# Residual add: from an accumulating transfer back to VectorE, with the first unit's PSUM copies moved from ScalarE to VectorE

## The chip, the cores and the metric

The kernel runs on one core of one Trainium2 chip. The metric is the device time of one execution in microseconds, as the median of repeated runs. Before the change it is 324.42 us (three runs, 323.83 to 324.49). The profile below is of one such execution with a span of 322.4 us.

The engines have short names in the profile: PE is TensorE (matmul), PEld its weight loads, DVE is VectorE, ACT is ScalarE, POOL is GpSimd, SP is SyncE. [...]

## What is computed

A gated linear attention over four batches of 768 tokens, eight heads of 48 channels, and behind it a gated feed-forward layer with a residual:

```
for t in range(S):                         # state S is complex, a is the complex decay
    S_re, S_im = a[t] * S + k[t] v[t]^T    # the outer product is real
    y[t] = q[t] . S_re
x   = y as (3072 tokens, 384)
out = x + sigmoid(x @ w_res) * ((gelu(x @ w_gate) * (x @ w_val)) @ w_out)
```

The kernel replaces the recurrence by chunks. The decay is brought to logarithm and angle, both are summed over time with triangular matmuls, and q and k are scaled by exp(+sum), exp(-sum), and by cosine and sine of the angle sum. Each chunk of 128 tokens is then ordinary masked attention plus a carried state.

## The kernel before

A group `g` is 256 tokens (two chunks, C = 2). A unit is one or two groups: unit 0 is group 0, unit 1 is groups 1 and 2, and so on to unit 6, which is group 11. The program alternates two phases. Phase x(u) makes the exponentials, angles and sines of unit u+1, the logarithm steps of unit u+2, the second half of the attention of unit u and the output products of unit u-1. Phase y(u) makes the gate and value products of unit u with gelu, and begins the attention of unit u+1.

`weave` sorts the steps of several lists by a fraction of the phase, so a pair such as `(0.75, 0.8, ...)` says where in the phase a list of steps lies. Every activation and every table load goes through `act` or `table`, which chain them in the order of the text:

```
def tab(ins):
    if "tab" in T:
        tc.add_manual_dep(ins.ins, T["tab"].ins.name, order, reason="table order")
    T["tab"] = ins
```

The angle sum is reduced to turns, and VectorE takes its absolute value for the cosine by clearing the sign bit:

```
# cs_t(g, c): cs holds the angle sum in PSUM, fg[..., 1, :] the fraction, fg[..., 0, :] its magnitude
nc.vector.tensor_scalar(out=r, in0=cs3, scalar1=MAGIC, scalar2=MAGIC, op0=OP.add, op1=OP.subtract)
nc.vector.tensor_tensor(out=fg[:, hs, 1, :], in0=cs3, in1=r, op=OP.subtract)
if c == C - 1:
    nc.vector.tensor_scalar(out=fg[:, :, 0, :].bitcast(int32), in0=fg[:, :, 1, :].bitcast(int32),
                            scalar1=0x7FFFFFFF, scalar2=None, op0=OP.bitwise_and)
# p2_sin(g): two ACT Sin passes over fg give CS; products(g): DVE makes Q and K from CS
```

Attention copies the transposed q and k out of PSUM, one half on each engine, and casts the result; `xt_step` copies its transpose (cuts marked):

```
nc.scalar.copy(out=qk[0:DD, 0:512], in_=tp[0:DD, 0:512])
nc.vector.tensor_copy(out=qk[0:DD, 512:1024], in_=tp[0:DD, 512:1024])
...
x = xp.tile([128, DM], BF, tag="x", name="x")
nc.scalar.copy(out=x, in_=y)
...
if jj % 2 == 0:
    nc.scalar.copy(out=dst, in_=src)          # xt_step
else:
    nc.vector.tensor_copy(out=dst, in_=src)
```

The output step, once for each chunk of 128 tokens:

```
def op_step(u, jj):
    ...                                       # 12 matmuls into ps
    nc.vector.scalar_tensor_tensor(out=ot, in0=T["sg", u][:, jj], scalar=1.0, in1=ps, op0=OP.add, op1=OP.mult)
    t0 = token(u, jj) * 128
    if u == NU - 1:
        nc.vector.tensor_tensor(out=ot, in0=ot, in1=T["x", token(u, jj)], op=OP.add)
    nc.sync.dma_start(out=out[t0:t0 + 128, :], in_=ot)
    if u < NU - 1:
        nc.gpsimd.dma_start(out=out[t0:t0 + 128, :], in_=T["x", token(u, jj)], accum_op=OP.add)
```

GpSimd's queue also carries the loads of v and of the weights, and a small round trip through DRAM that turns one row of decays into a column. `decay0` and `decay2` write a row (`dm<-ar`, `dm<-E`, `dm<-Ei`) and read it back as `m`; `decay3` then makes M from it on VectorE. Groups 5, 7, 8, 10 and 11 use it; groups 1, 2 and 4 use a matmul instead.

The order of steps in the first phase x, which the change touches:

```
if u == 0:
    weave((0.0, 0.25, p1 of g1), (0.26, 0.3, csls), (0.31, 0.32, sm[0]), (0.35, 0.45, exs),
          (0.4, 0.64, p1 of g2), (0.641, 0.642, dec3), (0.645, 0.65, atn[:1]),      # atn[0] loads the table
          (0.65, 0.66, arctan of g1), (0.67, 0.85, cst), (0.75, 0.8, atn[1:]),      # atn[1:] is arctan of g2
          (0.9, 0.95, sin of g1), (0.96, 0.97, sm[1]), (0.0, 0.5, att))
```

Here g1 is the second unit (groups 1 and 2) and g2 the third (groups 3 and 4).

Of the kernel before, what the change touches and what calls it, by code (L numbers as in the profile page):

```python
# [12 lines left out]
OP = mybir.AluOpType  # L13
# [15 lines left out]
def kernel(  # L29
# [13 lines left out]
    nc = tc.nc  # L43
# [70 lines left out]
    T = {}  # L114
# [114 lines left out]
    def cs_t(g, c):  # L229
        s = g % NS  # L230
        th = T["th", g]
        if c == 0:
            T["fg", g] = pE.tile([128, C * H, 2, D], FP, tag="fg", name="fg")
        sl = slice(c * DM, (c + 1) * DM)
        cs = psM.tile([128, DM], FP, tag="mm", padded_shape=[128, 512], name="cst")
        nc.tensor.matmul(out=cs, lhsT=tmat[c], rhs=th[:, sl], start=True, stop=(s == 0))  # L236
        if s > 0:
            nc.tensor.matmul(out=cs, lhsT=ones2pi, rhs=T["P", g], start=False, stop=True)
        cs3 = cs.rearrange("p (h d) -> p h d", h=H)
        fg = T["fg", g]  # L240
        hs = slice(c * H, (c + 1) * H)
        r = pS.tile([128, H, D], FP, tag="r", name="r")
        nc.vector.tensor_scalar(out=r, in0=cs3, scalar1=MAGIC, scalar2=MAGIC, op0=OP.add, op1=OP.subtract)
        nc.vector.tensor_tensor(out=fg[:, hs, 1, :], in0=cs3, in1=r, op=OP.subtract)
        if c == C - 1:
            nc.vector.tensor_scalar(out=fg[:, :, 0, :].bitcast(mybir.dt.int32), in0=fg[:, :, 1, :].bitcast(mybir.dt.int32),  # L246
                                    scalar1=0x7FFFFFFF, scalar2=None, op0=OP.bitwise_and)

    def p2_sin(g):
        T["CS", g] = pQ.tile([128, C * H, 2, D], BF, tag="CS", name="CS")  # L250
# [76 lines left out]
    def attention(g, c):  # L327
        s = g % NS
        first = s == 0 and c == 0
        st = {}  # L330

        def Q(x):
            return T["Q", g][:, x].rearrange("p u d -> p (u d)")

        def K(x):
            return T["K", g][:, x].rearrange("p u d -> p (u d)")

        def V(h):
            return T["v", g][:, c, h]

        def grp(hg):
            def a():
                tp = psT.tile([128, 1024], BF, tag="tp", name="tp")
                for j in range(4):
                    x = c * H + hg * 4 + j
                    nc.tensor.transpose(out=tp[0:DD, j * 128:j * 128 + 128], in_=Q(x), identity=ident)  # L346
                for j in range(4):
                    x = c * H + hg * 4 + j
                    nc.tensor.transpose(out=tp[0:DD, 512 + j * 128:640 + j * 128], in_=K(x), identity=ident)  # L349
                qk = sqp.tile([128, 1024], BF, tag="qk", name="qk")  # L350
                nc.scalar.copy(out=qk[0:DD, 0:512], in_=tp[0:DD, 0:512])  # L351
                nc.vector.tensor_copy(out=qk[0:DD, 512:1024], in_=tp[0:DD, 512:1024])  # L352
                st["qk", hg] = qk
                at = psA.tile([128, 4, 128], FP, tag="at", name="at")
                for j in range(4):
                    nc.tensor.matmul(out=at[:, j], lhsT=qk[0:DD, 512 + j * 128:640 + j * 128],  # L356
                                     rhs=qk[0:DD, j * 128:j * 128 + 128], start=True, stop=True)
                atm = sqp.tile([128, 4, 128], BF, tag="atm", name="atm")
                nc.vector.tensor_tensor(out=atm, in0=at, in1=mask4, op=OP.mult)  # L359
                st["atm", hg] = atm  # L360
            return a

        def enter():
            if s == 0 or c > 0:
                return
            d = T["dk", g - 1][0:DD].rearrange("p (h d) -> p h d", h=H)
            Mb = T["M", g][0:DD].rearrange("p (h u) -> p h u", u=1).to_broadcast([DD, H, D])
            G = stt.tile([128, H, D], FP, tag="G", name="G")
            if s == 1:
                nc.vector.tensor_tensor(out=G[0:DD], in0=d, in1=Mb, op=OP.mult)  # L370
            else:
                nc.vector.tensor_tensor(out=G[0:DD], in0=d, in1=T["G"][0:DD], op=OP.add)
                nc.vector.tensor_tensor(out=G[0:DD], in0=G[0:DD], in1=Mb, op=OP.mult)
            Gb = stt.tile([128, H, D], BF, tag="Gb", name="Gb")
            nc.vector.tensor_copy(out=Gb[0:DD], in_=G[0:DD])
            T["G"] = G
            T["Gbf"] = Gb

        def dk():
            if s == NS - 1 and c == C - 1:  # L380
                return
            if c == 0:
                T["dk", g] = psD.tile([128, DM], FP, tag="dk", padded_shape=[128, 512], name="dk")
            d = T["dk", g]
            for h in range(H):
                nc.tensor.matmul(out=d[0:DD, h * D:(h + 1) * D], lhsT=K(c * H + h), rhs=V(h),
                                 start=(c == 0 and h == 0), stop=(h == H - 1), skip_group_check=True)

        def yy():
            y = psY.tile([128, DM], FP, tag="y", padded_shape=[128, 512], name="y")  # L390
            for h in range(H):
                ys = y[:, h * D:(h + 1) * D]
                hg, j = divmod(h, 4)
                nc.tensor.matmul(out=ys, lhsT=st["atm", hg][:, j], rhs=V(h), start=True, stop=first)  # L394
                if not first:
                    nc.tensor.matmul(out=ys, lhsT=st["qk", hg][0:DD, j * 128:j * 128 + 128],
                                     rhs=T["Gbf"][0:DD, h], start=False, stop=True)
            x = xp.tile([128, DM], BF, tag="x", name="x")
            nc.scalar.copy(out=x, in_=y)
            T["x", g * C + c] = x  # L400
            if c == 0:
                d = T["dk", g][0:DD].rearrange("p (h d) -> p h d", h=H)
                Gb = stt.tile([128, H, D], BF, tag="Gb", name="Gb")
                if s == 0:
                    nc.vector.tensor_copy(out=Gb[0:DD], in_=d)
                else:
                    nc.vector.tensor_tensor(out=Gb[0:DD], in0=d, in1=T["G"][0:DD], op=OP.add)
                T["Gbf"] = Gb

        def hi(f):  # L410
            def w():
                with tc.high_priority():
                    f()
            return w
        return [hi(f) for f in (enter, grp(0), dk, grp(1), yy)]


    def xt_step(u, jj):
        if jj == 0:
            T["xT", u] = xtp.tile([128, KD, 512], BF, tag="xT", name="xT")[:, :, 0:width(u)]  # L420
        tpx = psM.tile([128, DM], BF, tag="mm", padded_shape=[128, 1024], name="tpx")
        x = T["x", token(u, jj)]
        for f in range(KD):
            nc.tensor.transpose(out=tpx[:, f * 128:(f + 1) * 128], in_=x[:, f * 128:(f + 1) * 128], identity=ident)
        dst = T["xT", u][:, :, jj * 128:(jj + 1) * 128]
        src = tpx.rearrange("p (f t) -> p f t", f=KD)
        if jj % 2 == 0:
            nc.scalar.copy(out=dst, in_=src)
        else:
            nc.vector.tensor_copy(out=dst, in_=src)  # L430
# [28 lines left out]
    def op_step(u, jj):  # L459
        h2 = T["h2", u]  # L460
        ps = psM.tile([128, DM], FP, tag="mm", padded_shape=[128, 512], name="op")
        for ffi in range(KF):
            nc.tensor.matmul(out=ps, lhsT=h2[:, ffi, jj * 128:(jj + 1) * 128], rhs=wo[:, ffi, :],  # L463
                             start=(ffi == 0), stop=(ffi == KF - 1))
        ot = ob.tile([128, DM], FP, tag="ot", name="ot")
        nc.vector.scalar_tensor_tensor(out=ot, in0=T["sg", u][:, jj], scalar=1.0, in1=ps, op0=OP.add, op1=OP.mult)  # L466
        t0 = token(u, jj) * 128
        if u == NU - 1:
            nc.vector.tensor_tensor(out=ot, in0=ot, in1=T["x", token(u, jj)], op=OP.add)
        nc.sync.dma_start(out=out[t0:t0 + 128, :], in_=ot)  # L470
        if u < NU - 1:
            nc.gpsimd.dma_start(out=out[t0:t0 + 128, :], in_=T["x", token(u, jj)], accum_op=OP.add)  # L472


    def table(nm):
# [7 lines left out]
    def token(u, jj):  # L483
        return UNITS[u][0] * C + jj
# [23 lines left out]
    def phase_x(u):  # L508
# [34 lines left out]
        if u == 0:  # L543
            sm = [[call(sums, g) for g in gg if g % NS > 0] for gg in (g1, g2)]
            weave((0.0, 0.25, zip_steps([p1(g) for g in g1])), (0.26, 0.3, csls), (0.31, 0.32, sm[0]), (0.35, 0.45, exs),
                  (0.4, 0.64, zip_steps([p1(g) for g in g2])), (0.641, 0.642, dec3), (0.645, 0.65, atn[:1]),
                  (0.65, 0.66, [call(p1_arctan, g) for g in g1]), (0.67, 0.85, cst), (0.75, 0.8, atn[1:]),
                  (0.9, 0.95, sin), (0.96, 0.97, sm[1]), (0.0, 0.5, att))
            return
        if u == 1:  # L550
# [80 lines left out]
```

## Time and profile before

| what | value |
|---|---|
| time, median of 3 | 324.42 us |
| span of the profiled execution | 322.4 us |
| mean granted TensorE clock | 0.949 |
| DMA traffic | 34.55 MB, mean 107 GB/s |
| HBM read, written | 31.31 MB, 9.07 MB |
| accumulating transfers `out_dram<-x` | 22, 192 KB each, 3.7 us from issue to landing |
| stores `out_dram<-ot` | 24, 192 KB each, 2.5 us from issue to landing |

Busy time says how long an engine worked in a stretch, not whether the end waited for it. A stage's limit is read from what its engines waited for last. In a group's row the last column is the idle time of that engine just before those instructions, with the event that ended it. In the chain of waits each row is a start, a length and what the end of the program hung on at that moment. A timeline row gives start, duration, engine, line, operation, output and inputs, and in brackets the idle time before it. Instructions on one engine overlap a little in their records, so the distance from start to start, and not the duration, is what one more instruction takes from a busy engine.

### The profile page before, as it was taken

What the parts mean: (1) busy time and instruction counts of PE and PEld (TensorE: products, weight loads), DVE (VectorE), ACT (ScalarE), POOL (GpSimd) and SP (SyncE); (2) the same over time, 40 slices, a digit from 0 to 9 for tenths busy, and PEclk for the clock granted to TensorE, in tenths of its full rate; (3) what the DMA queues carried; (4) which work ended last, traced back from release to release, by engine and by line L of the source; (5) the groups of instructions that cost most, each with busy time, mean ns of one, the idle gap of its engine ahead of it and who ended that gap; (6) DMA issues with size and microseconds to landing.
All of it is one profiled execution on the core that took longest, in us unless ns stands there. A gap on an engine that the chain in (4) does not pass through costs nothing.

```text
span 322.4 us, 5853 instructions
## 1 busy us (share of the span) xinstructions
PE 272.1 (84%) x2200; PEld 170.5 (53%) x2200; DVE 234.8 (73%) x431; ACT 209.8 (65%) x353; POOL 80.5 (25%) x115
## 2 busy tenths in 40 slices
PE   0337927789887999789997999998999999899994
PEld 0116624677543666445664556554656655555682
DVE  2446769968499995599982999974899837864352
ACT  4549684646998557977568976569665683656150
POOL 1206522022040370259020572000630003200220
PEclk9995676959999999999999999999999999999998
DMA  8999999989999995396850595000360003600441
GB/s 159 218 183 181 182 169 165 185 174 180 187 179 186 223 160 33 76 197 113 122 36 2 107 121 95 2 0 3 75 122 3 2 0 76 122 2 0 107 91 50
DMA packets 137755, 34.55 MB, mean 107 GB/s; under 512 B 126848, under 2 KB 137728, under 8 KB 137728
## 3 DMA queue, kind: packets, MB, share of 16 engines
q1 hardware_dynamic: 103296, 23.60, 36.8%
q0 software_dynamic: 34432, 10.59, 31.2%
q8 instruction: 17, 0.28, 0.3%
q14 instruction: 10, 0.08, 0.1%
HBM read 31.31 MB, written 9.07 MB: 125 GB/s over the span
## 4 chain that ended last, share of the span: by engine, by line
PE 56%; SPq 12%; ACT 11%; DMA 9%; DVE 6%; issue 3%; POOL 1%; ACTq 0%; DVEq 0%; POOLq 0%
PE vp L443 14%; PE gp L439 13%; SPq L136 6%; SPq L144 6%; PE op L463 6%; DMA k<-in_k_dram 4%; PE rp L455 3%; PE tp L349 3%; PE tp L346 3%; PE at L356 3%; ACT L477 3%; DMA m<-dm 3%; ACT s L124 3%; PE cst L236 2%; PE y L394 2%
## 5 line engine op out<-in xcount | busy, mean ns | idle before, releaser
L124 ACT ACTIVATE h<-gp 128x512 bf16<-128x512 f32 (+1 forms) x84 | 44.5, 536 | 38.4 <-PE gp L439 37.9
L439 PE MATMUL gp<-xT,wg 128*128 128x512 bf16 (+1 forms) x252 | 65.4, 353 | 3.4 <-ACT h L124 2.0
L443 PE MATMUL vp<-xT,wv 128*128 128x512 bf16 (+1 forms) x252 | 66.6, 353 | 0.0
L446 DVE SCALAR_TENSOR_TENSOR h<-h,vp 128x512 bf16<-128x512 bf16 (+1 forms) x84 | 49.8, 603 | 16.4 <-PE vp L443 12.0
L463 PE MATMUL op<-wo,h 128*128 128x384 bf16 x288 | 50.2, 326 | 8.1 <-ACT Ei L124 5.9
L463 PEld LDWEIGHTS <-h 128*128 128x128 bf16 x288 | 27.8, 98 | 28.7 <-issue 11.3
L351 ACT COPY qk<-tp 96x512 bf16<-96x512 bf16 x48 | 27.9, 580 | 17.1 <-PE tp L349 7.9
L359 DVE TENSOR_TENSOR atm<-at,mask 128x512 bf16<-128x512 f32 x48 | 32.9, 686 | 8.2 <-PE at L356 7.8
L472 POOL DMA_DIRECT2D out_dram<-x x22 | 20.4, 947 | 54.4 <-DMA out_dram<-ot 43.1
L439 PEld LDWEIGHTS <-wg 128*128 128x128 bf16 x252 | 23.7, 99 | 17.9 <-issue 4.2
L443 PEld LDWEIGHTS <-wv 128*128 128x128 bf16 x252 | 23.8, 99 | 13.3
L189 DVE TENSOR_TENSOR ai<-s,ai 128x768 f32<-128x768 f32 x12 | 11.1, 955 | 23.6 <-ACT s L124 23.6
L477 ACT ACT_TABLE_LOAD x21 | 26.9, 1283 | 1.1 <-PEq L615 0.7
L346 PE MATMUL tp<-ident,Q 128*96 128x128 bf16 x192 | 20.1, 231 | 6.9 <-DVE Q L321 6.2
L346 PEld LDWEIGHTS <-Q 128*96 128x96 bf16 x192 | 17.4, 130 | 15.3 <-DVE Q L321 10.0
L124 ACT ACTIVATE CS<-fg,hpi 128x768 bf16<-128x768 f32 x12 | 11.2, 935 | 20.8 <-DVE fg L246 20.7
L150 POOL DMA_DIRECT2D v<-in_v_dram x24 | 21.9, 932 | 4.2 <-DMA v<-in_v_dram 1.3
L349 PE MATMUL tp<-ident,K 128*96 128x128 bf16 x192 | 22.3, 235 | 0.0
L236 PE MATMUL cst<-ai,lt0b 128*128 128x384 f32 x24 | 11.8, 577 | 11.7 <-ACT ai L124 11.0
L352 DVE COPY qk<-tp 96x512 bf16<-96x512 bf16 x48 | 19.8, 413 | 2.3 <-ACT qk L351 1.7
L212 PE MATMUL csl<-ar,lt0a 128*128 128x384 f32 x24 | 11.4, 562 | 10.8 <-DMA ar<-in_a_re_dram 10.8
L466 DVE SCALAR_TENSOR_TENSOR ot<-sg,op 128x384 f32<-128x384 f32 x24 | 13.1, 547 | 10.1 <-PE op L463 10.1
(85 smaller groups left out, 522.0 us busy)
## 6 DMA issues: line engine op xcount, KB each, us to landing
ar<-in_a_re_dram SPq DMA_DIRECT2D x24, 192.0 KB, 4.7
ai<-in_a_im_dram SPq DMA_DIRECT2D x24, 192.0 KB, 4.1
q<-in_q_dram SPq DMA_DIRECT2D x24, 192.0 KB, 3.8
k<-in_k_dram SPq DMA_DIRECT2D x24, 192.0 KB, 3.7
out_dram<-ot SPq DMA_DIRECT2D x24, 192.0 KB, 2.5
out_dram<-x POOLq DMA_DIRECT2D x22, 192.0 KB, 3.7
v<-in_v_dram POOLq DMA_DIRECT2D x24, 96.0 KB, 5.0
wg<-in_moe_w_gate_dram POOLq DMA_DIRECT2D x4, 288.0 KB, 11.4
```

The costliest lines, as they stand in the source:

```text
L124: tab(nc.scalar.activation(**kw))
L150: nc.gpsimd.dma_start(out=t[:, c], in_=rows(v, g, c))
L346: nc.tensor.transpose(out=tp[0:DD, j * 128:j * 128 + 128], in_=Q(x), identity=ident)
L349: nc.tensor.transpose(out=tp[0:DD, 512 + j * 128:640 + j * 128], in_=K(x), identity=ident)
L351: nc.scalar.copy(out=qk[0:DD, 0:512], in_=tp[0:DD, 0:512])
L359: nc.vector.tensor_tensor(out=atm, in0=at, in1=mask4, op=OP.mult)
L439: nc.tensor.matmul(out=gp, lhsT=wg[:, fi, ffi * 128:(ffi + 1) * 128], rhs=xT[:, fi, :], start=(fi == 0), stop=(fi == KD - 1))
L443: nc.tensor.matmul(out=vp, lhsT=wv[:, fi, ffi * 128:(ffi + 1) * 128], rhs=xT[:, fi, :], start=(fi == 0), stop=(fi == KD - 1))
L446: nc.vector.scalar_tensor_tensor(out=h2[:, ffi, :], in0=h2[:, ffi, :], scalar=0.5, in1=vp, op0=OP.mult, op1=OP.mult)
L463: nc.tensor.matmul(out=ps, lhsT=h2[:, ffi, jj * 128:(jj + 1) * 128], rhs=wo[:, ffi, :], start=(ffi == 0), stop=(ffi == KF - 1))
L472: nc.gpsimd.dma_start(out=out[t0:t0 + 128, :], in_=T["x", token(u, jj)], accum_op=OP.add)
L477: tab(nc.scalar.preload_act_table_set(nm))
```

## The change

It has four parts.

- The residual x of units 0 to 5 is added on VectorE before the store, as unit 6 did already, in place of an accumulating transfer behind the store. This takes 22 transfers off GpSimd's queue.
- The absolute value of the fraction is max(-f, f) by one `scalar_tensor_tensor`, in place of clearing the sign bit by an integer `tensor_scalar`.
- For group 0, VectorE takes the copies of q, of x and of xT out of PSUM that ScalarE did. This is to relieve ScalarE at the start.
- In phase x(0) the arctangents of the third unit stand behind the sines of the second.

The result is the same as before in each part.

```
-            nc.vector.tensor_scalar(out=fg[:, :, 0, :].bitcast(mybir.dt.int32), in0=fg[:, :, 1, :].bitcast(mybir.dt.int32),
-                                    scalar1=0x7FFFFFFF, scalar2=None, op0=OP.bitwise_and)
+            nc.vector.scalar_tensor_tensor(out=fg[:, :, 0, :], in0=fg[:, :, 1, :], scalar=-1.0, in1=fg[:, :, 1, :],
+                                           op0=OP.mult, op1=OP.max)
...
-                nc.scalar.copy(out=qk[0:DD, 0:512], in_=tp[0:DD, 0:512])
+                (nc.vector.tensor_copy if g <= FIRST else nc.scalar.copy)(out=qk[0:DD, 0:512], in_=tp[0:DD, 0:512])
...
-            nc.scalar.copy(out=x, in_=y)
+            (nc.vector.tensor_copy if g <= FIRST else nc.scalar.copy)(out=x, in_=y)
...
-        if jj % 2 == 0:
+        if jj % 2 == 0 and u > 0:
             nc.scalar.copy(out=dst, in_=src)
...
+        nc.vector.tensor_tensor(out=ot, in0=ot, in1=T["x", token(u, jj)], op=OP.add)
         t0 = token(u, jj) * 128
-        if u == NU - 1:
-            nc.vector.tensor_tensor(out=ot, in0=ot, in1=T["x", token(u, jj)], op=OP.add)
         nc.sync.dma_start(out=out[t0:t0 + 128, :], in_=ot)
-        if u < NU - 1:
-            nc.gpsimd.dma_start(out=out[t0:t0 + 128, :], in_=T["x", token(u, jj)], accum_op=OP.add)
...
-                  (0.65, 0.66, [call(p1_arctan, g) for g in g1]), (0.67, 0.85, cst), (0.75, 0.8, atn[1:]),
+                  (0.65, 0.66, [call(p1_arctan, g) for g in g1]), (0.67, 0.85, cst), (0.98, 0.99, atn[1:]),
```

## Prediction, made before the changed kernel was run

> **What bounds the kernel now.** I began with the busy times of the page.
>
> ```profile
> PE 272.1 (84%) x2200; PEld 170.5 (53%) x2200; DVE 234.8 (73%) x431; ACT 209.8 (65%) x353; POOL 80.5 (25%) x115
> ```
>
> TensorE leads, but a mean says little about stages, so I cut the span at the table loads (phase x opens with the logarithm table, phase y with gelu) and asked for busy time in each stretch. The columns are the stretch, its length, and the busy time (with the count) of PE, PEld, DVE, ACT and POOL, then clock, DMA share and GB/s.
>
> ```profile
> 147.00:173.00 26.00, 25.89 (x265) 16.04 (x263) 22.87 (x41) 16.91 (x31) 8.62 (x9) 1.00 0.61 77
> 173.00:192.00 19.00, 16.54 (x80) 9.22 (x78) 13.68 (x27) 16.57 (x27) 10.05 (x15) 1.00 0.52 80
> 192.00:219.00 27.00, 26.87 (x275) 16.40 (x275) 23.96 (x44) 17.32 (x32) 2.47 (x3) 1.00 0.25 40
> ```
>
> In phase y (first and third row) TensorE has no gap: that time is fixed by matmuls the change does not touch. In phase x (second row) no engine is full over the whole, so something is handed from engine to engine. VectorE's timeline there shows it: it sits idle for 5.13 us until ScalarE's first exponentials arrive at 177.6, and from then to the next phase y runs without a gap except one of 0.73 us. Its last rows:
>
> ```profile
> 189.31 0.16 DVE L282 TENSOR_TENSOR M<-m 96x8 f32<-96x8 f32 x1 [0.73 <-DMA m<-dm]
> 189.39 0.55 DVE L244 TENSOR_TENSOR fg<-cst,r 128x384 f32<-128x384 f32 x1
> 189.86 0.54 DVE L466 SCALAR_TENSOR_TENSOR ot<-sg,op 128x384 f32<-128x384 f32 x1
> 190.32 0.55 DVE L246 TENSOR_SCALAR fg<-fg 128x768 int32<-128x768 int32 x1
> ...
> 191.21 0.95 DVE L321 TENSOR_TENSOR Q<-CS,qE 128x1536 bf16<-128x1536 bf16 x1
> ```
>
> The magnitude (L246) releases the last sines, they release the gelu table load, and with it the first gelu; Q releases the transposes of attention. Whatever stands ahead of these on VectorE delays phase y. The chain of waits for the same stretch shows the other thread, the decay's round trip through DRAM, that makes the 0.73:
>
> ```profile
> 181.54 3.43 DMA dm<-Ei
> ...
> 185.25 0.79 POOL m L265
> 186.05 3.16 DMA m<-dm
> ...
> 189.31 0.10 DVE M L282
> ```
>
> The last view is ScalarE's timeline in the first phase x:
>
> ```profile
> 49.34 3.04 ACT L124 ACTIVATE ai<-ai 128x768 f32<-128x768 f32 x4
> 57.58 0.94 ACT L124 ACTIVATE CS<-fg,hpi 128x768 bf16<-128x768 f32 x1 [5.20 <-DVE fg L246]
> 60.98 0.94 ACT L124 ACTIVATE CS<-fg,hpi 128x768 bf16<-128x768 f32 x1 [1.73 <-DVE fg L246]
> 63.24 1.28 ACT L477 ACT_TABLE_LOAD   x1
> ```
>
> Four arctangents run in a row, two for the second unit and two for the third, and then ScalarE is idle for 5.2 us. The third unit's two are free where they stand.
>
> **Prices, from the groups by line.**
>
> ```profile
> L246 DVE TENSOR_SCALAR fg<-fg 128x768 int32<-128x768 int32 x12 | 6.7, 558 | 0.0
> L197 DVE SCALAR_TENSOR_TENSOR ar<-s,ar 128x768 f32<-128x768 f32 x12 | 11.3, 951 | 3.3 <-ACT s L124 3.3
> L469 DVE TENSOR_TENSOR ot<-ot,x 128x384 f32<-128x384 f32 x2 | 1.1, 558 | 0.1
> L472 POOL DMA_DIRECT2D out_dram<-x x22 | 20.4, 947 | 54.4 <-DMA out_dram<-ot 43.1
> L351 ACT COPY qk<-tp 96x512 bf16<-96x512 bf16 x48 | 27.9, 580 | 17.1 <-PE tp L349 7.9
> L352 DVE COPY qk<-tp 96x512 bf16<-96x512 bf16 x48 | 19.8, 413 | 2.3 <-ACT qk L351 1.7
> ```
>
> L469 is the residual add as the last unit does it already, and L197 has the form and size that the new magnitude gets, so both prices are measured here. On a busy VectorE one more instruction costs its distance from start to start: L466 to L246 above are 0.46 apart, two L197 of the other timeline rows (182.03 to 182.90) 0.87.
>
> [...] the accumulating issues stand on POOL, 947 ns each, in the queue that the decay's round trip uses. [...] Moving arctangents behind sines adds no load, since none lies between them in the rows above.
>
> **The change part by part.**
>
> *Residual adds.* 22 adds at 0.47 us are 10.3 us of VectorE. Unit 0's two fall in phase x(1), units 1 to 4 have four each in x(2) to x(5), and unit 5's four come at about 299 to 305, where VectorE waits 1.3 to 2.3 us for each output product: these last cost nothing. In the other phases most stand ahead of the last magnitude. By the timelines the output products ahead of it are one in x(1), three in x(2), three in x(3), three in x(4). I assume that each add follows its product directly.
>
> *Magnitude.* 0.87 - 0.47 = 0.40 us, 12 times, 4.8 us in all, always ahead of the sines it releases. Two fall in each phase that prepares two groups.
>
> *Round trip.* With no accumulation in GpSimd's queue, m should land earlier. The three waits of M on m sum to 3.4 us: 0.73 in x(3), 1.00 in x(4), 1.64 in x(5). VectorE arrives later as well, so I take those of x(3) and x(4) as gone.
>
> Sums for the delay of phase y: x(1) 0.47 + 0.80 = 1.3; x(2) 3 x 0.47 + 0.80 = 2.2, with no wait to absorb it; x(3) 2.2 - 0.7 = 1.5; x(4) 2.2 - 1.0 = 1.2; x(5), one group, with two adds hidden in the 1.64 us gap and one in a 0.73 us gap ahead of Q, 0.4 for the magnitude and some 0.2 of the add ahead of K, 0.6. Together 6.8 us.
>
> *First unit.* Seven copies leave ScalarE: four of q, two of x, one of xT, by start distances 4 x 0.46 + 3 x 0.38 = 3.0 us. The waits for TensorE that they made (0.53, 0.84, 0.52, 0.16, 0.55) sum to 2.6. VectorE takes 4 x 0.34 + 2 x 0.47 + 0.27 = 2.6 us more, in the stretch from 30 to 63 us where it is already busy for 26.84 of 33. The logarithms of the second unit come about 1 us sooner, but the exponentials behind them wait for cumulative sums that need VectorE and TensorE. I credit 1.5 us of the possible 5.6.
>
> *Arctangents and magnitude in the opening.* The two moved arctangents, 1.5 us by start distance, go from a free place to directly ahead of the gelu table load at 63.24: +1.5. Three magnitudes before phase y(0): +1.2. With the credit the opening is +1.2.
>
> The sum is 6.8 + 1.2 = 8.0 us, or 332.4. VectorE gets 10.3 + 4.8 + 2.6 = 17.7 us in all, so this charges 45% of it. Programs usually hide a little more than a reading by hand finds, as the instruction order is drawn up anew, so I place the prediction at 331.2.
>
> **Rivals.**
>
> 1. *GpSimd's queue was the true limit of phase x.* For it: in x(3) dm<-Ei takes 3.43 us against a median of 1.6, with an accumulation issued just behind it; in x(4) the chain itself passes through L472 for 0.54 us. Against it: all waits for m come to 3.4 us, and x(2) has none. Then VectorE's extra is largely absorbed, and the time is 323 to 327.
> 2. *The opening pays all of its 5.6 us.* For it: ScalarE runs nearly without a gap from 24.6 to 48 us. Against it: VectorE fills up, and the moved arctangents take 1.5 back. It would give about 328.
> 3. *VectorE becomes the bound.* It is busy for 23 to 24 of 26 to 27 us in phase y, so a backlog carried over meets little slack. Charging 70% of 17.7 us gives 336.8.
> 4. *Transfers.* They are near saturation to about 120 us (DMA digits 8 and 9), and 4.3 MB of accumulation go, but from 105.9 us on, where compute waits for hardly any load. Worth 0 to 1 us.
>
> **Range and chances.** Predicted 331.2 us, range 325.5 to 336.5. Two percent above 324.42 is 330.9, almost at my centre: slower by over 2% 0.53, within 2% 0.45, faster by over 2% 0.02.
>
> **What the changed profile would show.** L246 at about 950 ns, 24 adds at 558 ns, VectorE near 253 us busy; no L472, and the waits of M for m gone in x(3) and x(4). Phases x(1) to x(4) longer by 1 to 2 us each, phases y as long as before. In the opening the logarithms of the second unit about 1 us earlier, two arctangents directly ahead of the second gelu-side table load, and phase y(0) later by about 1 us. The prediction is wrong if the adds are scheduled behind Q and the last magnitude, if the round trip's earlier landing shortens phase x by more than its visible waits, or if the opening gains several microseconds because ScalarE alone held it.

## The result and the profile after

The changed kernel takes 329.64 us (four runs, 328.67 to 330.57) against 324.46 us before, a ratio of 1.0161 with a 95% interval of 1.0126 to 1.0195: about 5.2 us longer, inside the predicted range and 1.6 us below its centre. Ratios here and below leave out executions of over 1.5% above the fastest of their kernel. The likelier of the two outcomes named, slower by over 2%, did not come. The total came out near, but several of the terms that it was summed from did not; they are taken one by one below.

The busy times of the page after, in the same columns as before:

```profile
PE 272.9 (83%) x2200; PEld 170.8 (52%) x2200; DVE 251.5 (77%) x460; ACT 205.6 (63%) x346; POOL 58.5 (18%) x93
```

VectorE went from 234.8 to 251.5 us with 29 more instructions, GpSimd from 80.5 to 58.5 with the 22 transfers gone, and ScalarE lost seven instructions. TensorE has the same 2200 matmuls. The groups by line show the prices:

```profile
L467 DVE TENSOR_TENSOR ot<-ot,x 128x384 f32<-128x384 f32 x24 | 13.2, 550 | 0.2
L246 DVE SCALAR_TENSOR_TENSOR fg<-fg 128x768 f32<-128x768 f32 x12 | 11.4, 949 | 0.1
L282 DVE TENSOR_TENSOR M<-m 96x8 f32<-96x8 f32 x5 | 0.7, 154 | 0.9 <-DMA m<-dm 0.8
```

The add costs 550 ns, the magnitude 949 where it was 558, and M now waits 0.8 us in all for m, where it waited 3.4 (what ended these waits is taken up below).

For the place of the loss I cut both spans at the table loads again. The first two rows are phases x(2) and y(2) of the kernel before, the next four are x(2), y(2), x(3) and y(3) after; columns as in the prediction.

```profile
127.84:147.02 19.18, 15.92 (x79) 8.72 (x78) 14.26 (x27) 17.04 (x26) 8.25 (x13) 1.00 0.61 125
147.02:173.00 25.98, 25.87 (x265) 16.04 (x263) 22.85 (x41) 16.91 (x30) 8.60 (x9) 1.00 0.61 77
```

```profile
130.89:151.58 20.69, 16.26 (x80) 8.71 (x78) 16.21 (x29) 17.04 (x26) 8.61 (x13) 1.00 0.52 107
151.58:177.13 25.55, 25.49 (x263) 15.92 (x262) 23.18 (x43) 16.29 (x30) 2.66 (x4) 1.00 0.48 55
177.13:197.92 20.79, 17.64 (x85) 9.85 (x84) 16.20 (x32) 17.14 (x27) 8.37 (x13) 1.00 0.53 78
197.92:224.28 26.36, 25.93 (x272) 16.07 (x270) 23.95 (x43) 16.51 (x31) 0.00 (x0) 1.00 0.03 9
```

Phase x(2) is 1.51 us longer and VectorE is busy 1.95 us longer in it. Phase y(2), which the prediction held constant, is 0.43 us shorter. TensorE is busy 0.34 us more in x(2) and 0.38 less in y(2): while phase x drags on, TensorE goes ahead with the gate and value products (1.66 us of them in x(2), where it was 1.38), and phase y has less left to do. The same subtraction for all phases, in us:

| | 1 | 2 | 3 | 4 | 5 | sum |
|---|---|---|---|---|---|---|
| phase x, predicted | 1.3 | 2.2 | 1.5 | 1.2 | 0.6 | 6.8 |
| phase x, measured | 1.40 | 1.51 | 1.20 | 0.27 | 0.61 | 4.99 |
| phase y, measured | -0.37 | -0.43 | 0.00 | -0.06 | -0.45 | -1.31 |

So 3.7 us come from phases x(1) to y(5). The two profiled executions differ by 5.4 us in their spans: 2.0 us lie ahead of x(1), and 0.3 us are gained behind y(5). Taken from the timed 5.2 us, 1.5 us are left for the opening, so it cost 1.5 to 2 us.

VectorE's timeline near the end of x(3) after shows how the additions delay phase y:

```profile
193.87 0.54 DVE L466 SCALAR_TENSOR_TENSOR ot<-sg,op 128x384 f32<-128x384 f32 x1
194.33 0.54 DVE L244 TENSOR_TENSOR fg<-cst,r 128x384 f32<-128x384 f32 x1
194.79 0.54 DVE L467 TENSOR_TENSOR ot<-ot,x 128x384 f32<-128x384 f32 x1
195.26 0.94 DVE L246 SCALAR_TENSOR_TENSOR fg<-fg 128x768 f32<-128x768 f32 x1
...
196.86 0.22 DVE L282 TENSOR_TENSOR M<-m 96x8 f32<-96x8 f32 x2
```

No row has a wait; M finds its m landed. The add (L467) stands between its product and the magnitude, 0.47 us from start to start where its record lasts 0.54, and the magnitude takes 0.87 to the next start where its record lasts 0.94. But the add stands two places behind its product, not directly behind as assumed. In x(4) the last one so falls behind the magnitude:

```profile
238.80 0.54 DVE L466 SCALAR_TENSOR_TENSOR ot<-sg,op 128x384 f32<-128x384 f32 x1
239.26 0.95 DVE L246 SCALAR_TENSOR_TENSOR fg<-fg 128x768 f32<-128x768 f32 x1
240.13 0.55 DVE L467 TENSOR_TENSOR ot<-ot,x 128x384 f32<-128x384 f32 x1
```

### The profile page after: what moved, and what is told of

It is laid out like the page before. It is cut to its first block, busy times and chain, and to the rows that moved or that the text cites. A ratio compares the mean times of both kernels' runs of the same rounds, so it can differ in the third digit from the quotient of the medians.

```text
span 327.8 us, 5827 instructions
## 1 busy us (share of the span) xinstructions
PE 272.9 (83%) x2200; PEld 170.8 (52%) x2200; DVE 251.5 (77%) x460; ACT 205.6 (63%) x346; POOL 58.5 (18%) x93
## 5 line engine op out<-in xcount | busy, mean ns | idle before, releaser
L439 PE MATMUL gp<-xT,wg 128*128 128x512 bf16 (+1 forms) x252 | 66.6, 351 | 6.0 <-DVE xT L430 3.7
L443 PE MATMUL vp<-xT,wv 128*128 128x512 bf16 (+1 forms) x252 | 64.8, 351 | 0.0
L351 ACT COPY qk<-tp 96x512 bf16<-96x512 bf16 x44 | 25.5, 580 | 18.4 <-PE tp L349 11.8
L474 ACT ACT_TABLE_LOAD x21 | 26.9, 1283 | 1.1 <-PEq L612 0.7
L346 PEld LDWEIGHTS <-Q 128*96 128x96 bf16 x192 | 16.7, 129 | 17.7 <-DVE Q L321 10.3
L356 PE MATMUL at<-qk 96*128 96x128 bf16 x192 | 19.8, 228 | 0.0
L394 PEld LDWEIGHTS <-atm 128*128 128x128 bf16 x192 | 13.0, 99 | 12.1 <-DVE atm L359 10.9
```

The costliest lines, as they stand in the source:

```text
L351: (nc.vector.tensor_copy if g <= FIRST else nc.scalar.copy)(out=qk[0:DD, 0:512], in_=tp[0:DD, 0:512])
L439: nc.tensor.matmul(out=gp, lhsT=wg[:, fi, ffi * 128:(ffi + 1) * 128], rhs=xT[:, fi, :], start=(fi == 0), stop=(fi == KD - 1))
L443: nc.tensor.matmul(out=vp, lhsT=wv[:, fi, ffi * 128:(ffi + 1) * 128], rhs=xT[:, fi, :], start=(fi == 0), stop=(fi == KD - 1))
L474: tab(nc.scalar.preload_act_table_set(nm))
```

## The experiments

All differences below are the measured ratio less one, times the median of the kernel before on the same chip (323.88 to 324.39 us). A ratio is not the quotient of the two medians, from which it can differ by up to 1.1 us. The brackets behind a ratio are its 95% interval.

The profiled executions of the parts lie below their medians: 324.53 us for the adds alone, 324.29 for the magnitude alone, and 323.42, the fastest of 22, for the copies alone, against medians of 326.20, 325.59 and 325.27. Their spans are 0.3, 0.0 and -0.8 us longer than that of the kernel before. The phases show what a part does to each stage, but they do not add up to the medians, and a share of each loss is not located. Where a change lies in the opening alone, single phases from x(1) to y(5) still differ from the kernel before by up to 0.4 us, but for one execution taken up below.

### The four parts alone

**The adds alone**, the transfers being gone with them:

```
+        nc.vector.tensor_tensor(out=ot, in0=ot, in1=T["x", token(u, jj)], op=OP.add)
-        if u < NU - 1:
-            nc.gpsimd.dma_start(out=out[t0:t0 + 128, :], in_=T["x", token(u, jj)], accum_op=OP.add)
```

> Kernel before with only the residual adds on VectorE in place of the accumulating transfers. Theory A (VectorE's instruction stream ahead of the last magnitude and of Q sets phase x): the adds ahead of it cost 0.5 us in x(1), 1.4 in x(2), 1.4 less the vanished waits for m in x(3) and x(4), 0.2 in x(5), together about 3 us of which phases y give back up to 0.9: plus 2 to 3 us. Rival B (GpSimd's queue held phase x, the relief pays for the adds, and the loss lies in the opening): 0 us, between minus 1 and plus 0.7.

Measured: 326.20 us, ratio 1.0057 (1.0039 to 1.0075), +1.85 us. This is just below the range of Theory A and clear of that of Rival B.

**The magnitude alone:**

```
-            nc.vector.tensor_scalar(..., scalar1=0x7FFFFFFF, scalar2=None, op0=OP.bitwise_and)
+            nc.vector.scalar_tensor_tensor(..., scalar=-1.0, in1=fg[:, :, 1, :], op0=OP.mult, op1=OP.max)
```

> Kernel before with only the magnitude as max(-f, f), 0.40 us longer each, 12 times, always ahead of a sine. Theory A: 0.8 us in each of x(1) and x(2), 0.4 in x(5), less in x(3) and x(4) where waits for m of 0.7 and 1.0 us take it up, and 1.2 in the opening, of which phase y(0) gives a part back: plus 2 to 3.5 us. Rival B: the opening alone shows it, plus 0 to 1 us.

Measured: 325.59 us, ratio 1.0053 (1.0032 to 1.0074), +1.7 us. Phases x(1) to x(5) are longer by 0.87, 0.75, 0.63, 0.39 and 0.40, in all 3.0 us, near the 3.6 that the prediction has for them (four times 0.8, and 0.4). Phases y give back 1.9. The remaining 0.6 or so of the 1.7 us is not located, and the total lies between the ranges of Theory A and of Rival B.

**The seven copies alone:**

```
-                nc.scalar.copy(out=qk[0:DD, 0:512], in_=tp[0:DD, 0:512])
+                (nc.vector.tensor_copy if g <= FIRST else nc.scalar.copy)(out=qk[0:DD, 0:512], in_=tp[0:DD, 0:512])
...   # and so for x and xT
```

> Kernel before with only the seven PSUM copies of the first unit moved to VectorE. Theory A (in the changed kernel's profile the stretch from the logarithm table to the trigonometric table became 2.1 us longer, since VectorE runs the copies ahead of the decay steps that the cumulative sums and the exponentials wait for): plus 1 to 2.5 us at the table load, of which phase y(0) gives most back, so plus 0.3 to 1.5 us at the end. Rival C (the copies relieve ScalarE as intended and the 2.1 us come from the slower clock granted to TensorE in that profile, 0.56 against 0.64): minus 0.5 to minus 2 us.

Measured: 325.27 us, ratio 1.0038 (1.0024 to 1.0051), +1.2 us. As Theory A has it, the part that was meant to bring time costs time. ScalarE's timeline of this kernel:

```profile
28.07 0.84 ACT L124 ACTIVATE s<-ai 128x768 f32<-128x768 f32 x1 [0.93 <-DVE ai L189]
30.70 0.84 ACT L124 ACTIVATE s<-ai 128x768 f32<-128x768 f32 x1 [1.78 <-DVE ai L189]
31.45 1.56 ACT L124 ACTIVATE s<-s 128x768 f32<-128x768 f32 x2
38.25 0.49 ACT L124 ACTIVATE E<-csl 128x384 f32<-128x384 f32 x1 [5.25 <-PE csl L212]
```

The relief is gone before the logarithms (`s<-s`): ScalarE waits 0.93 and 1.78 us for `ai`, which VectorE makes between the copies, and the logarithms start 8.65 us after the logarithm table, where they started after 7.31. ScalarE is free at 33.0 and then waits 5.25 us for the sums of logarithms. Before, four copies stood between the logarithms and the first exponential; the last of them and the exponential were:

```profile
35.20 0.48 ACT L428 COPY xT<-tpx 128x384 bf16<-128x384 bf16 x1 [0.16 <-PE tpx L424]
36.59 0.49 ACT L124 ACTIVATE E<-csl 128x384 f32<-128x384 f32 x1 [0.91 <-PE csl L212]
```

The freed time became a wait, and a longer one: VectorE, which makes `ar` for these sums from the second unit's `s`, has the copies and masks of attention ahead of it:

```profile
33.64 0.68 DVE L359 TENSOR_TENSOR atm<-at,mask 128x512 bf16<-128x512 f32 x1
34.24 0.34 DVE L430 COPY xT<-tpx 128x384 bf16<-128x384 bf16 x1
34.50 0.94 DVE L197 SCALAR_TENSOR_TENSOR ar<-s,ar 128x768 f32<-128x768 f32 x1
```

**The order of the arctangents alone:**

```
-                  (0.65, 0.66, arctan of g1), (0.67, 0.85, cst), (0.75, 0.8, atn[1:]),
+                  (0.65, 0.66, arctan of g1), (0.67, 0.85, cst), (0.98, 0.99, atn[1:]),
```

> Kernel before with only the third unit's arctangents behind the second unit's sines. Theory A: 1.5 us more ahead of the gelu table load, of which phase y(0), whose TensorE work can be rearranged, gives back at least half: plus 0 to 0.8 us at the end. Rival D (the moved arctangents clear the way for the second unit's sines): minus 0.5 to minus 1.5 us.

Measured: 324.51 us, ratio 1.0006 (0.9991 to 1.0021), +0.2 us. In its profile the gelu table comes 2.29 us later against the load before it, and y(0) is 2.05 us shorter. TensorE's clock was nearly the same in the two stretches y(0), 0.83 before and 0.82 here; but attention ran further ahead of the gelu table: the second of its `qk` copies on ScalarE comes 0.58 us before that load, where it came 1.30 us behind it.

The four parts alone sum to 1.85 + 1.7 + 1.2 + 0.2 = 4.95 us, near the 5.2 of the whole. Their intervals put about 1 us of doubt on that sum.

### What the adds cost, and what the transfers cost

**No residual for units 0 to 5:** neither add nor transfer. The kernel leaves the residual of these units out of its output.

```
-        if u < NU - 1:
-            nc.gpsimd.dma_start(out=out[t0:t0 + 128, :], in_=T["x", token(u, jj)], accum_op=OP.add)
```

> Kernel before without the residual of units 0 to 5 altogether: no accumulating transfer and no add on VectorE (the output lacks x there). What it gains on the kernel before is the price of the accumulating transfers, and what the first experiment stands above it is the price of the adds. Theory A (the transfers cost only through the waits of M for m in x(3) to x(5), 3.4 us of VectorE's idle time, part of them needed anyway): minus 0.5 to minus 2 us. Rival B (GpSimd's queue held phase x): minus 3 us or more. Rival E (the transfers are wholly hidden): minus 0.3 to plus 0.3.

Measured: 322.63 us, ratio 0.9957 (0.9945 to 0.9969), -1.4 us, of which the profile shows 0.63 in x(4); the rest is not located. So the transfers held back 1.4 us, and the adds themselves cost 1.85 + 1.4 = 3.25 us, with some 0.7 us of doubt from the two intervals. The waits of M for m are still 2.5 of the 3.4 us here, the longest of them 1.6 as before.

**Transfers kept, but queued behind the round trip.** Is it the traffic of 4.3 MB that costs, or the place in GpSimd's queue? This kernel is the one before, with the same accumulations put in the program's text at the start of the next phase y and kept behind a read-back of `m`:

```
-            nc.gpsimd.dma_start(out=out[t0:t0 + 128, :], in_=T["x", token(u, jj)], accum_op=OP.add)
+            late.append(lambda: nc.gpsimd.dma_start(out=..., in_=..., accum_op=OP.add))
...
+        with (tc.issue_after(T["turned"].ins) if "turned" in T else ExitStack()):   # first step of phase y
+            for f in late:
+                f()
```

> Kernel before with the accumulating transfers kept, but queued on GpSimd behind the decay's round trip of their phase. Leaving the residual out gained 1.4 us. If this gain was the queue (an accumulation ahead of the transfer that brings m), most of it comes here: minus 0.7 to minus 1.4 us. If it was the traffic of the accumulations or their share of GpSimd's time, nothing: minus 0.3 to plus 0.3 us.

Measured: 322.62 us, ratio 0.9959 (0.9942 to 0.9977), -1.3 us. This is nearly all of the 1.4, with every byte still moved. GpSimd's timeline in x(4), first of the kernel before, then of this one:

```profile
227.45 0.91 POOL L472 DMA_DIRECT2D out_dram<-x  x1 [0.27 <-DMA dm<-Ei]
228.25 0.89 POOL L265 DMA_DIRECT2D m<-dm  x1
229.02 0.61 POOL L262 DMA_DIRECT2D dm<-ar  x1
229.51 0.88 POOL L265 DMA_DIRECT2D m<-dm  x1
```

```profile
227.18 1.51 POOL L265 DMA_DIRECT2D m<-dm  x2 [0.57 <-DMA dm<-Ei]
228.68 0.52 POOL L262 DMA_DIRECT2D dm<-ar  x1
229.19 0.96 POOL L472 DMA_DIRECT2D out_dram<-x  x1
```

Before, one issue of an accumulation stands ahead of the reads of `m`; here the first two reads go out ahead of it, though later accumulations still stand ahead of the last two, and x(4) is 0.65 us shorter. The second of these reads, for which M waits, goes out 1.83 us after the issue of `dm<-E`, where it went out after 2.81: 0.5 of the 1.0 us between is the accumulation, and 0.5 a `dm<-ar` that stood between the two reads. It lands no faster for that: it took 3.26 us, and 2.95 before. So in x(4) the queue order was the cost, not the traffic; the other 0.7 us are not located. By the two ratios this version beats both kernels, with 1.3 us below the one before and some 6.5 us below the changed one.

### Do adds and magnitude hinder each other?

> Kernel before with the adds and the magnitude together, the opening's two parts left out. If both are plain charges on VectorE's stream they add up: 1.85 + 1.7 = plus 3.5 us. If each alone was partly paid out of the same idle time (the waits for m in x(3) and x(4)), both together cost more than the sum: plus 4.2 to 5 us.

Measured, both parts together: 330.46 us (six runs, 326.42 to 331.49), ratio 1.0153 (1.0104 to 1.0203), +5.0 us, where the sum of the two alone is 3.55. A second measurement of the same kernel was to decide between the two answers:

> The sixth experiment once more (adds and magnitude together), since its interval of plus 3.4 to 6.6 us holds both answers. By the stages of the profiles, phases x add up exactly (x(1) to x(5): 1.39, 1.51, 1.20, 0.09, 0.47 together, against 1.47, 1.71, 1.19, 0.09, 0.51 as sums), but phases y give back 1.3 us together against 0.8 and 1.9 alone: if y's slack is one reserve that is spent once, plus 4.2 to 5 us; if the two add up, plus 3.2 to 3.8 us.

Measured: 326.67 us (six runs, 326.30 to 331.89), ratio 1.0113 (1.0069 to 1.0156), +3.65 us. The times lie partly near 326.5 and partly above 330 us, and the intervals of the two measurements overlap. In the phases the two profiles agree: x(1) to x(5) are longer by 1.40, 1.52, 1.20, 0.08 and 0.61 in the second, where the two parts alone sum to 1.47, 1.71, 1.19, 0.09 and 0.51. So the delays in phase x add up. In phase y they give back 1.3 us together, but 0.8 and 1.9 alone; a reserve that can be spent only once would fit that. Whether the total exceeds the sum stays open. Both profiles are of executions near 326.5 us, so they do not show what lengthens the others.

### Where the opening loses

Four kernels were to find what the copies' 1.2 us hang on. First theory: the steps of the second unit's decay stand behind the copies on VectorE. So these steps and their sums got priority, with the copies on VectorE and, as a control, on ScalarE:

```
-            nc.vector.scalar_tensor_tensor(out=lm, in0=T["s", g], scalar=0.5, in1=lm, op0=OP.mult, op1=OP.add)
+            with (tc.high_priority(10000) if g in UNITS[1] else ExitStack()):
+                nc.vector.scalar_tensor_tensor(out=lm, in0=T["s", g], scalar=0.5, in1=lm, op0=OP.mult, op1=OP.add)
...   # and so for the other decay steps and the matmul of csl
```

> The third experiment (seven copies on VectorE) with one thing more: the second unit's decay steps on VectorE and its cumulative sums on TensorE get a higher priority, so that they stand ahead of the copies and of the masks where they are ready. Theory A (the copies cost time because VectorE runs them, and the attention that they speed up, ahead of the decay steps that ScalarE's exponentials wait for): the loss of 1.2 us is gone, minus 1.5 to plus 0.3 us against the kernel before. Rival F (two halves of qk copied one after the other on one engine hold TensorE up): still plus 0.8 to 1.5 us.

> Kernel before with only that higher priority, the copies left on ScalarE. Theory A: the decay steps do not wait long for VectorE here (they start within 0.1 us of ScalarE's logarithm), so little is gained: minus 0.8 to plus 0.3 us. Were the order as such worth as much as in the kernel with the copies, minus 1.5 us or more.

Measured: 326.78 us, ratio 1.0070 (1.0048 to 1.0092), +2.3 us with the copies moved; 327.38 us, ratio 1.0108 (1.0077 to 1.0139), +3.5 us without. The theory fell, and both losses are larger than any range given. With the copies moved, the steps are done at 33.7 us, but the sums wait on TensorE, where attention stands ahead of them. TensorE's timeline of the first:

```profile
34.40 0.66 PE L349 MATMUL tp<-ident,Q 128*96 128x128 bf16 x4 [2.24 <-DVE qk L355]
...
36.75 1.59 PE L215 MATMUL csl<-ar,lt0a 128*128 128x384 f32 x2
```

The transposes wait 2.24 us for a `qk` copy that now comes behind the decay steps on VectorE, and the sums wait for the transposes and for what follows them. Second theory, then: it is the order on TensorE. The sums go ahead of the last two attention groups, again with the copies moved and not moved:

```
+        T["csl"] = nc.tensor.matmul(out=cs, lhsT=lmat[c], rhs=T["lm", g][:, sl], start=True, stop=True)
...
+                    with (tc.issue_after(T["csl"].ins) if g == FIRST and c == 1 and hg == 0 else ExitStack()):
...
-                  (0.9, 0.95, sin), (0.96, 0.97, sm[1]), (0.0, 0.5, att))
+                  (0.9, 0.95, sin), (0.96, 0.97, sm[1]), (0.31, 0.75, att))
```

> The third experiment (seven copies on VectorE) with TensorE's order changed: the second unit's cumulative sums stand ahead of the last two attention groups of the first unit, not behind them. Theory G (in the opening ScalarE's exponentials wait for cumulative sums that stand behind attention on TensorE's queue; each instruction of attention that VectorE gets, or is kept from, delays them, which is why moving copies to VectorE lost 1.2 us and moving decay steps ahead lost 2.3 and 3.5): with the sums ahead, the wait of 5.25 us of the first exponential shrinks to 2 to 3 us and the relief of ScalarE shows, minus 1 to minus 2.5 us against the kernel before, so 2 to 3.5 below the third experiment. Rival (the attention put off is itself needed as early, for x and the gate products): plus 0 to 1.5 us.

> Kernel before with only that order on TensorE, the copies left on ScalarE. Theory G: the sums come earlier here too, but the copies that ScalarE still makes for the attention put off stand between its exponentials: minus 0.5 to minus 1.5 us, less gain than with the copies on VectorE. Rival: plus 0 to 1.5 us.

Measured: 324.98 us, ratio 1.0023 (1.0007 to 1.0039), +0.7 us with the copies moved; 326.13 us, ratio 1.0049 (1.0022 to 1.0075), +1.6 us without. In this order, then, having the copies on VectorE looks the cheaper, but no gain on the kernel before appears. The comparison is weak: the times of the second spread from 323.12 to 329.23 us, and in its profiled execution, the longest, 3.4 us of the excess lie in x(5) and y(5), far from the change. In x(5) ScalarE waited 4.27 us for the magnitude, where it waited 2.45 before, and 3.09 us in all for TensorE between the first and the third gelu of y(5), where it waited 1.60; what held VectorE and TensorE up is not shown. ScalarE's timeline of the first shows where the gain goes:

```profile
35.72 0.49 ACT L124 ACTIVATE E<-csl 128x384 f32<-128x384 f32 x1 [2.73 <-PE csl L212]
...
45.52 0.84 ACT L124 ACTIVATE s<-ai 128x768 f32<-128x768 f32 x1 [2.29 <-DVE ai L189]
47.25 0.84 ACT L124 ACTIVATE s<-ai 128x768 f32<-128x768 f32 x1 [0.88 <-DVE ai L189]
```

The wait for the sums fell from 5.25 to 2.73 us, as the theory has it. But the attention groups put off so now stand ahead of the third unit's `ai` on VectorE, and ScalarE waits there:

```profile
43.95 0.68 DVE L360 TENSOR_TENSOR atm<-at,mask 128x512 bf16<-128x512 f32 x1
44.55 0.94 DVE L189 TENSOR_TENSOR ai<-s,ai 128x768 f32<-128x768 f32 x1
```

The trigonometric table is loaded at 49.77, against 49.39 with the copies alone. The loss moved with the order and was not removed; which single instruction the 1.2 us hang on is not settled.

## Why the prediction was right, and where its steps were not

- **The bound.** The reading that phase x hands its time from engine to engine and that VectorE's tail there sets phase y held. The adds and the magnitude charge it, at 0.47 and 0.40 us each, as priced. One reading was loose: 182.03 to 182.90 is the distance from an L197 to the L244 behind it, not between two L197; the 0.87 us stand.
- **Residual adds.** Mis-sized. Those of phases x(1) to x(5) were put at about 4.9 us on the path; the adds against no residual at all cost 3.25. By the phases of these two profiles they take 0.87, 0.98, 0.60, 0.32 and 0.13 us, 2.9 in all, where the steps have 0.47, three times 1.41 and 0.2. The assumption that each add follows its product directly failed: it comes two places later, and in x(4) the last falls behind the last magnitude. That is 0.47 us; the rest of what x(4) lacks (1.2 predicted, 0.27 measured) is not explained by it. In x(1) the new order also brought a second output product ahead of the last magnitude.
- **Magnitude.** Right in phase x (3.0 measured, 3.6 predicted), but its net cost is 1.7 of the 4.8 us charged. Phases y(1) to y(5) give 1.9 back. The opening, where 1.2 was charged, is 0.9 us shorter in that profile, with y(0) at a higher clock (0.91 against 0.83), so nothing can be read there of the charge.
- **Round trip.** Its waits for m vanished in x(3) and x(4) as expected, but mostly for the second reason given, that VectorE arrives later: without the transfers alone they fall from 3.4 to 2.5 us only, and in x(3) M's step now stands behind the last magnitude. That the 1.7 us credited are close to the 1.4 that leaving the transfers out brings is in part luck. Rival 1, GpSimd's queue as the limit, was true in this amount and no more: it named 323 to 327 us for the whole change. Its sign in x(3) misled: the reads of m go out 3.71 us after the issue of `dm<-Ei` with an accumulation in between, and 4.04 us after it in the changed kernel, which has none.
- **"Phases y as long as before".** This step failed. They give back 1.3 us; in y(2), where it was followed, because "TensorE has no gap" in phase y does not mean that its work must all be done there: 0.28 us of the gate and value products moved ahead into x(2).
- **First unit's copies.** The wrong sign: -1.5 credited, +1.2 measured alone. The logarithms of the second unit did not come 1 us earlier but 1.3 us later against their table load, in this kernel and in the changed one, as ScalarE waits for `ai` from the fuller VectorE. The sentence that the exponentials wait for sums that need VectorE and TensorE was the right doubt; the mistake was to credit anything for an engine whose next instruction would wait.
- **Arctangents.** Charged 1.5, measured 0.2 alone. They now stand ahead of the gelu load as expected, with one copy in between, and there are 21 table loads of 1283 ns each in the kernel before and in the changed one; but the later gelu load cost nearly nothing at the end: y(0) was shorter by almost as much, as attention ran ahead of the load, at an unchanged clock. In the changed kernel y(0) is also 1.67 us shorter, but at a clock of 0.91 in place of 0.83, so there it is not shown.
- **The opening's sum.** +1.2 predicted, 1.5 to 2 found, and that it is so near is luck, by errors that cancel: the copies were 2.7 us too low and the arctangents 1.3 too high. With 1.2 and 0.2 for these, 0.1 to 0.6 is left for the three magnitudes in place of 1.2; terms as small as this the runs don't resolve.
- **The total.** 8.0 us by the steps, 6.8 after the discount for what programs hide, 5.2 measured. The discount was a guess in the right direction; its content is the 1.3 us given back in phase y and the 1.8 too many in phase x.
- **The other rivals.** That the opening pays fell with the copies alone. VectorE as the bound at 336.8 did not come. That fewer bytes bring time fell with the deferred transfers, which keep the bytes and have the gain.

## What to carry to other kernels

Before relieving an engine, look up what its next instructions wait for. Here ScalarE's first exponential waited for sums that need the engine that took the copies over, and with the copies gone its wait grew from 0.91 to 5.25 us. A transfer that waits on a store can cost little by its bytes and still delay a small transfer queued behind it: leaving the 22 accumulations out gained 1.4 us, and moving them back in the queue, with every byte kept, gained 1.3. Try a transfer's place in the queue before moving its work to a busy engine, where the adds cost 3.25 us. When a stage is made later, look whether a neighbour can take over some of its work before charging the whole delay: here phases x became 5.0 us longer, and phases y gave 1.3 of them back.

## What was not expected of the hardware

TensorE's granted clock in the opening differs between executions of one and the same kernel. The clock row of the page, 40 slices of the span, for the two runs of adds and magnitude together:

```profile
PEclk9995776989999999999999999999999999999999
```

```profile
PEclk9955676979999999999999999999999999999999
```

A slice is 8.1 us. In the first row the clock falls to half in the fourth slice, in the second already in the third; in stretches of 2 us it stands at 0.50 from 24 to 36 us in the first and from 18 to 36 us in the second. What sets the moment of the fall is not shown, nor why the clock stays at half from 24 to 38 us in the changed kernel, with TensorE 60 to 84% busy in every 2 us of it. Phase y(0) differs with the clock: it took 20.28 us at a mean clock of 0.83 in the kernel before, and 18.94 us at 0.91 in the kernel with the adds alone, whose change begins behind it. From these 1.34 us I estimate that stage times ahead of 75 us from a single profile carry some 1 to 1.5 us of chance: the profile of the copies alone ends 0.4 us earlier at the last table load than that of the kernel before, while its timed median is 1.2 us longer. The opening was therefore judged by medians, and only the later phases, at clock 1.00, by stage.
